# Retention and two Strassen MLPs: unit pairs read and combined a stage sooner, words loaded as staging frees, attention in halves

## The chip, the core and the metric

One core of a Trainium2 chip. TensorE multiplies, VectorE and ScalarE move and convert, GpSimd (POOL) and SyncE (SP) issue DMAs, each in its own order. The metric is the device time of one execution, in microseconds (us): lower is better.

## What is computed

The input of 4 batches, 8 heads, 768 positions and a head size of 64 goes through a retention (a linear attention with a decay per head), then two MLPs over 3072 tokens of width 512 with a hidden width of 2048, all in fp32:

```python
for t in range(S):
    state = gamma * state + einsum('bhd,bhe->bhde', k[:, :, t], v[:, :, t])
    y[:, :, t] = scale * einsum('bhd,bhde->bhe', q[:, :, t], state)
x = y.transpose(0, 2, 1, 3).reshape(B * S, H * D)
h = x @ w_in1;  x = np.maximum(0.01 * h, h) @ w_out1
h = np.maximum(x @ w_in2, 0.0);  return (h * h) @ w_out2
```

The weights come as 64-bit words (the doubles that numpy holds) and are turned into fp32 on the chip.

## The kernel before, in words

**Numbers.** Every fp32 operand is held as a high and a low part, and every product takes three matmuls (high by high, low by high, high by low): `product` (line 692) is 6 matmuls, for two tiles of depth. Tokens go in three blocks of 1024, each in two halves of 512.

**Phase one: retention, first block.** The launch runs 8 attention units. Then `begin_loop` (1141) and `plain_period(q)` (1189, q from 2 to 7) work through the 8 pairs of hidden blocks of the first layer. A period runs `emit_plain` (739, the products into the hidden layer, evacuated at line 720) and `put_out` (1120, which is 12 matmuls of `emit_out`, 768). Beside that it converts the words of the weights: `load_w` (316) loads 1 MB of them (w_in: two tiles tagged `sg`; w_out: two tiles in `xh2`, `xl2` or `xh7`, `xl7`), `scale_words` (367) makes two ScalarE passes, `shift`, `sign` and `add` (372 to 384) three VectorE passes, and `add` is the last to read the words. `combine` (444) forms the seven units of a pair (4 in tile wa: units 1, 5, 6, 3; 3 in tile wb: 7, 2, 4), and they are kept in HBM as `wid`. Each period from q = 3 also holds one attention unit (`group`, 1134).

`attend` (204) does the scores of one unit and the output of the unit before it: 16 pairs of small score matmuls mixed with the first half of `y`, then the increments mixed with the second half of `y`. `y` has one bank in PSUM after the launch; line 276 (VectorE) empties it and line 256 takes the scores. `group` then loads q, k and v (tiles `r`) for later units.

**The late loop** (1413) runs the 16 `emit_out` of the second token half, with a `group()` behind i = 0, 2, 5 and 8, `split_late(i + 2)` (splitting hidden tiles into `gh`, `gl` or `gg`) ahead, and words of w2, in 512 KB pieces (tiles `st`, `load_piece` 334): pieces 0 to 2 are loaded ahead of the loop, the rest by `next_piece` (1125), which also converts one piece.

**Phase two: Strassen.** Block 1 runs `strassen_period`. Blocks (0, 2), (1, 0), (1, 1) and (1, 2) (layer, block) run `both_block` (922). For each pair n it runs `first_half` (859: products 1, 5, 6, 3, with the banks `pa` and `pd` copied out by ScalarE at lines 865, 868, 871 and by VectorE at 874) and, between them, `second_half` of the pair before (878: products 7, 2, 4). The order on TensorE is 1, 7, 5, 2, 6, 4, 3, where 7, 2 and 4 belong to the pair before. Product 6 adds to the bank of product 1, and product 3 to that of product 5. `first_half` needs wa alone, `second_half` wb alone. `read_units` (808) loads both for pair n + 1 at the end of pair n; each has two buffers.

Then come seven stages of 48 matmuls (`STAGES`, order 1, 5, 6, 3, 7, 2, 4; n is the stage's number from 0, e its entry from 0 to 15), while VectorE and ScalarE prepare the next stage (`prepare`), and `read_stage` loads the weights of the stage after. Block (0, 2) also combines pairs 0 and 1 of the second layer there: `units_here` (811) loads the fp32 weights through POOL's queue (`store`), combines them in two steps and stores the units; pair 0 begins at (n, e) = (1, 1), pair 1 at (2, 13), both in the tile `xh4`. `operands` (664) prepares the seven operands of the next block in steps at the entries of the table `at`; its last read of `xs` frees that tile, into which block (1, 0) then loads (`made`, line 929, through SP).

**What sets the order.** TensorE's order is the order written (`mm` chains every matmul behind the last one). With `strict` on, so is that of VectorE and ScalarE (`seq`); the late loop and `both_block` are not strict, and there a list scheduler of the framework places the instructions, but within `aside()` (111) an instruction stays behind the last marked one. `load` issues on SP, `store` on POOL; both queues work in order, and an issue that waits for a tile holds up those behind it. A tile's next load waits until its last reader is done.

Of the kernel before, what the change touches and what calls it, by code (L numbers as in the profile page):

```python
# [17 lines left out]
P = 128  # L18
# [39 lines left out]
def retention_then_two_mlps(  # L58
# [74 lines left out]
    def mm(**kw):  # L133
        pin(nc.tensor.matmul(**kw))  # L134

    def load(**io):
        pin(nc.sync.dma_start(**io))  # L137

    def store(**io):
        pin(nc.gpsimd.dma_start(**io))  # L140
# [60 lines left out]
            return state[:, j + 1 - (c > 0)]  # L201
        return sts[n][:, k - 1]

    def attend(score=True, behind_mask=None):

        n = n_score[0] if score else NA
        m = n_done[0] if n_done[0] < n_score[0] else -1
# [36 lines left out]
        for one, two in (runs[0:2], runs[2:4]):  # L244
            for i in range(0, len(sets), 2):
                for kw in one[i:i + 2] + two[i:i + 2]:
                    mm(**kw)
        if n < NA:
            if c == 0:
                both = x_p.tile([P, 2, T], F32, tag=("xh7", "xl7", "xh2", "xl2")[n % 4], name="pm")  # L250
                pms[n] = both[:, 0]
                sts[n] = both[:, 1].rearrange("p (k b e) -> p k b e", k=4, b=2)
            else:
                pms[n] = a_p.tile([P, T], F32, tag="pm", name="pm", bufs=1)
                sts[n] = a_p.tile([P, 3, 2, D], F32, tag="st", name="st", bufs=1)
            seq(nc.vector.tensor_tensor(  # L256
                out=blocks(pms[n]), in0=blocks(sc), in1=mk[p].unsqueeze(1).to_broadcast([P, T // CH, CH]), op=ALU.mult,
            ))
            if c == 0:
                seq(nc.scalar.copy(memory(n, 1), inc[:, 0]))  # L260
# [55 lines left out]
    def load_w(q, half):  # L316
        if q >= NQ:
            return
        if half and q:
            t = [x_p.tile([P, 512], U64, tag=f"x{l}{2 if q % 2 else 7}", name="sg") for l in "hl"]  # L320
            for n in range(2):
                load(out=t[n], in_=w1[q, 1][:, 512 * n:512 * n + 512])
        else:
            t = w_p.tile([P, 1024], U64, tag="sg", name="sg", bufs=2)
            load(out=t, in_=w1[q, half])
        stage[q, half] = t
# [78 lines left out]
    def parts(t, k, n):  # L405
        return t.rearrange("p (k l n c) -> p k l n c", k=k, l=2, n=n)

    def put_in(lay, q, a, c):

        k = lay + 1  # L410
        a, c = parts(a, k, 4), parts(c, k, 3)
        win[lay, q] = {
            i: [
                [t[:, kt % k, l, m, kt // k * P:kt // k * P + P] for l in range(2)]
                for kt in range(2) for t, m in ((a, n - 3) if n >= 3 else (c, n),)
            ]
            for i, n in UNIT.items()
        }

    def open_in(q):  # L420

# [386 lines left out]
    def read_units(lay, q):  # L808
        read_wid(lay, q, *unit_tiles())

    def units_here(q, f, x=None):
        store(out=f, in_=wflt[q, 0])
        yield
        a, c = unit_tiles()
        put_in(1, q, a, c)
        steps = combine(f, a, c, 2, x)
        for _ in range(2 if x is None else 1):
            next(steps)
        if x is not None:
            put_wid(1, q, a, None)  # L820
        yield
        for _ in steps:
            pass
        put_wid(1, q, a if x is None else None, c)
# [97 lines left out]
    def both_block(lay, b, here):  # L922
# [4 lines left out]
        if here_too:  # L927
            v = quarters() + scratch("ss", "ss", "wb", "wf")
            made = make_units(5, *v[:5], put=load, apart=True)
            next(made)  # L930
        for n in range(NQ + 1):
            f = first_half(lay, b, n) if n < NQ else iter(())
            r = second_half(lay, b, n - 1, pa) if n else iter(())
            if here_too and 3 <= n <= 6:
                with aside():
                    next(here[n // 5], None)
            if here_too and n == NQ - 1:
                with aside():
                    next(made, None)
            for k in range(4):  # L940
                pa = next(f, None)
                if n == NQ - 1 and k < 2:
                    read_stage(lay, 0, (2 * k, 2 * k + 1))
                if lay == 0 and n and (k == 1 or k == 3 and n in (1, 2, 4, 5)):
                    with aside():
                        next(here, None)
                if k < 3:
                    next(r, None)
                if here_too and (n, k) in ((2, 0), (4, 0), (4, 2), (6, 0)):
                    with aside():  # L950
                        next(made, None)
            if n == NQ - 1:
                read_stage(lay, 1, range(4))
            if n and n + 1 < NQ and (not here_too or n not in (3, 5)):
                read_units(lay, n + 1)
            if here_too:
                if n in (1, 2, 4, 6):
                    with aside():
                        next(made, None)
                if n == 0:  # L960
                    here = [units_here(4, v[5], v[7]), units_here(6, v[6], v[5])]
                    for m in here:
                        next(m)
                elif n in (2, 4):
                    made = make_units(5 + n // 2, *v[:5], apart=True)
                    next(made)
        A = [ps["acc"].tile([P, T], F32, tag=f"acc{m}", name="acc") for m in range(2)]
        s = {}
        steps = None if nl is None else operands(nl, nb)
        at = {4: (7, 13), 5: (5, 11), 6: (1, 5, 9)} if lay else {4: (13,), 5: (5, 11), 6: (1, 4, 8, 12)}  # L970
        for n, i in enumerate(STAGES):
            if i in (5, 2):
                Dd = [ps["acc"].tile([P, T], F32, tag=f"acc{2 + m}", name="acc") for m in range(2)]
# [5 lines left out]
            for e, (q, m) in enumerate(order):  # L979
                r = rot[i, q]  # L980
                for k, (l, h) in enumerate(((0, 0), (1, 0), (0, 1))):
                    mm(
                        out=bank[m], lhsT=units[i, q // 2][:, q % 2, l, m * P:(m + 1) * P], rhs=r[:, h],
                        start=i in (1, 5, 2) and q == 0 and k == 0, stop=q == NQ - 1 and k == 2, skip_group_check=True,
                    )
                if e % 2 and n + 1 < len(STAGES):
                    prepare(STAGES[n + 1], q)
                if e == 1:
                    if 1 <= n <= 5:
                        read_stage(lay, n + 1, range(4))  # L990
                    if n == (1 if lay else 3) and nl is not None:
                        read_x(nb)
                    if n in (3, 5) and lay and nl is not None:
                        read_units(1, (n - 3) // 2)
                if lay == 0:
                    if (n, e) in ((0, 1), (0, 9), (0, 15)):
                        with aside():
                            next(here, None)
                    if (n, e) in ((1, 1), (2, 13)):
                        made = units_here(n - 1, x_p.tile([P, 1024], F32, tag="xh4", name="of"))  # L1000
                        next(made)
                    if n in (2, 4) and e in (3, 9):
                        with aside():
                            next(made, None)
                if steps and e in at.get(n, ()):
                    with aside():
                        next(steps, None)
# [123 lines left out]
            cast_piece(n)  # L1131
        n_piece[0] += 1

    def group():

        attend(n_score[0] < NA)
        n = n_score[0]
        value_loads_to(n + 1)
        loads_to(n + 2)

    def begin_loop(out):
# [14 lines left out]
        add(w, f)  # L1156
        store(out=wraw[2], in_=f)
        load_w(3, 0)
        o = hold_out(0)
        high_out(0, o)  # L1160
        low_out(0, o)
# [27 lines left out]
    def plain_period(q):  # L1189

        last = q == NQ - 1

        load_w(q + 2, 0)
        split_high(2 * q - 2)
        if not last:
            w, f = open_in(q + 1)
# [14 lines left out]
        if not last:  # L1211
            add(w, f)
            store(out=wraw[q + 1], in_=f)
        else:
            made = make_in(1, 0)
            next(made)
# [12 lines left out]
        for s, r in out:  # L1229
            add(s, r)  # L1230
        load_w(q + 2, 1)

        put_out(0, 2 * q - 2)
        if not last:
# [148 lines left out]
    for b in range(NB - 1):  # L1383
# [14 lines left out]
        if b == 0:  # L1398
            for _ in made:
                pass  # L1400
            sum_up(stage["of", NQ - 1])
            sums_high(NQ - 1)
            sums_low(NQ - 1)
            for n in range(3):
                load_piece(n)
        put_out(b, NJ - 2)
        put_out(b, NJ - 1)
        strict[0] = False
# [4 lines left out]
        for i in range(NJ):  # L1413
            if i + 2 < NJ:
                split_late(i + 2)
            emit_out(0, b, 1, 2 * LATE[i // 2] + i % 2, (0, 12), i == 0, i == NJ - 1)
            k = i // 2 + 3
            if i % 2 and k < NQ:
                read_out(LATE[k], spare if k % 3 == 2 else None)
            if b == 0 and i in (0, 2, 5, 8):  # L1420
                group()
                with aside():
                    prep_to(n_score[0] + 1)
            if b == 0 and i == 11:
# [98 lines left out]
```

## Time and profile before

| | us |
|---|---|
| median of 3 runs | 1061.63 (1057.16 to 1063.43) |
| profiled execution | 1057.65 |
| its span, first to last instruction | 1055.6 |

The profile is of that one execution. Times in its views are us from the span's start. PE is TensorE, DVE VectorE, ACT ScalarE; "L134" is line 134, where every matmul is recorded, so matmuls are told apart by their tiles. A wait names what ended it. The granted clock (PEclk) is a share of 2.4 GHz; over a stretch it is a mean of its two levels, 1.2 and 2.4.

### The profile page before, as it was taken

The page shows a single profiled execution, that of the slowest core. Times are in us where ns is not written, and L with a number is a line of the kernel's source. Part 1 is how long each engine was busy: PE and PEld are TensorE (multiplying, and loading weights), DVE is VectorE, ACT ScalarE, POOL GpSimd, SP SyncE. Part 2 cuts the span into 40 slices and gives each one's busy share as a digit, 9 for nine tenths or more (in the row PEclk, how much of TensorE's full clock was granted, in tenths as well). Part 3 has the DMA queues.
Part 4 walks back from the last instruction along what each step waited for, and adds up shares of the span by engine and source line. Part 5 has one row for each costly group of instructions (what it writes and reads, how often), then busy time and mean ns, then how long its engine had stood idle before and what let it go on. Part 6 is the DMA issues. An engine that isn't in the chain of part 4 may idle for free.

```text
span 1055.6 us, 18359 instructions
## 1 busy us (share of the span) xinstructions
PE 1026.1 (97%) x7133; PEld 842.1 (80%) x7133; DVE 764.4 (72%) x1273; ACT 586.0 (56%) x999; POOL 89.9 (9%) x155
## 2 busy tenths in 40 slices
PE   6899999899999999999999899999999999999998
PEld 5787888687877888887788688888888888888886
DVE  5796988777888759487888678868455958456953
ACT  4575664455566556476566466655455555455542
POOL 0010111101000000122011121001000001000000
PEclk8999999899999999999999999999999999999999
DMA  9688976998999878799896588975356784357461
GB/s 341 210 306 334 362 245 208 411 345 302 398 407 361 334 259 329 278 357 369 322 332 254 213 316 305 391 265 230 121 186 242 272 286 183 128 201 276 163 239 60
DMA packets 74277, 294.01 MB, mean 279 GB/s; under 512 B 8400, under 2 KB 8656, under 8 KB 63952
## 3 DMA queue, kind: packets, MB, share of 16 engines
q1 hardware_dynamic: 55536, 213.08, 55.6%
q0 software_dynamic: 18512, 79.70, 19.3%
q8 instruction: 56, 0.92, 0.3%
q14 instruction: 29, 0.24, 0.1%
q10 hardware_dynamic: 144, 0.07, 0.0%
HBM read 206.84 MB, written 85.98 MB: 277 GB/s over the span
## 4 chain that ended last, share of the span: by engine, by line
PE 84%; DMA 10%; DVE 3%; ACT 1%; SPq 1%; issue 1%; ACTq 0%; DVEq 0%
PE acc L134 43%; PE pa L134 25%; PE pd L134 9%; PE pb L134 5%; DMA wa<-wid 2%; DMA wf<-wraw 2%; DMA r<-first 2%; DMA st<-w 2%; DMA sg<-w 1%; PE y L134 1%; PE sc L134 1%; SPq L137 1%; DMA wo<-wpl 1%; PE inc L134 1%; DVE wa L396 0%
## 5 line engine op out<-in xcount | busy, mean ns | idle before, releaser
L134 PE MATMUL acc<-rot,wu 128*128 128x512 f32 x1344 | 308.3, 391 | 0.0
L134 PEld LDWEIGHTS acc<-rot,wu 128*128 128x128 f32 x1344 | 252.4, 188 | 55.3
L134 PE MATMUL pa<-xh,wa 128*128 128x512 f32 x576 | 180.1, 394 | 9.2 <-DMA wa<-wid 4.9
L847 DVE TENSOR_TENSOR rot<-gu,rot 128x512 fp32r<-128x512 f32 x160 | 109.3, 688 | 47.5 <-ACT rot L846 47.1
L846 ACT CAST rot<-gu 128x512 fp32r<-128x512 f32 x160 | 99.4, 621 | 77.0 <-PE acc L134 53.6
L134 PEld LDWEIGHTS pa<-xh,wa 128*128 128x128 f32 x576 | 107.8, 189 | 34.4 <-DMA wa<-wid 6.1
L134 PE MATMUL pa<-xl,wa 128*128 128x512 f32 x288 | 112.7, 391 | 0.0
L134 PE MATMUL acc<-gh,wo 128*128 128x512 f32 x400 | 104.8, 394 | 0.1
L134 PE MATMUL pa<-xh,wb 128*128 128x512 f32 x320 | 99.8, 393 | 0.5 <-DVE gt L881 0.5
L134 PE MATMUL pd<-xh,wa 128*128 128x512 f32 x320 | 98.5, 389 | 0.0
L134 PEld LDWEIGHTS acc<-gh,wo 128*128 128x128 f32 x400 | 74.5, 188 | 17.1 <-ACT gh L731 0.5
L134 PEld LDWEIGHTS pa<-xh,wb 128*128 128x128 f32 x320 | 59.5, 189 | 13.6 <-DVE gt L881 1.1
L134 PEld LDWEIGHTS pd<-xh,wa 128*128 128x128 f32 x320 | 60.1, 188 | 12.5
L847 DVE TENSOR_TENSOR rot<-gt,rot 128x512 fp32r<-128x512 f32 x64 | 44.1, 691 | 29.4 <-ACT rot L846 29.0
L134 PEld LDWEIGHTS pa<-xl,wa 128*128 128x128 f32 x288 | 54.3, 189 | 11.5
L134 PE MATMUL pa<-xl,wb 128*128 128x512 f32 x160 | 62.3, 389 | 0.0
L134 PE MATMUL pd<-xl,wa 128*128 128x512 f32 x160 | 62.2, 389 | 0.0
L846 ACT CAST rot<-gt 128x512 fp32r<-128x512 f32 x64 | 39.8, 622 | 38.7 <-DVE rot L847 27.1
L134 PE MATMUL acc<-gl,wo 128*128 128x512 f32 x200 | 56.8, 391 | 0.0
L711 ACT ACTIVATE gt<-gt 128x512 f32<-128x512 f32 x48 | 30.3, 632 | 45.3 <-DVE gt L874 32.5
L886 DVE TENSOR_TENSOR gu<-gu,pb 128x512 f32<-128x512 f32 x32 | 22.0, 687 | 41.3 <-PE pb L134 41.2
L134 PE MATMUL pb<-xh,wb 128*128 128x512 f32 x160 | 49.5, 391 | 0.8 <-DVE pm L256 0.8
(133 smaller groups left out, 1676.1 us busy)
## 6 DMA issues: line engine op xcount, KB each, us to landing
wu<-wou SPq DMA_DIRECT2D x100, 512.0 KB, 5.7
wa<-wid SPq DMA_DIRECT2D x28, 1024.0 KB, 7.3
wou<-of POOLq DMA_DIRECT2D x48, 512.0 KB, 6.7
wb<-wid SPq DMA_DIRECT2D x28, 768.0 KB, 5.9
wo<-wpl SPq DMA_DIRECT2D x20, 1024.0 KB, 7.9
r<-first SPq DMA_DIRECT2D x64, 256.0 KB, 8.0
st<-w SPq DMA_DIRECT2D x24, 512.0 KB, 9.0
wid<-wa POOLq DMA_DIRECT2D x12, 1024.0 KB, 8.9
```

The costliest lines, as they stand in the source:

```text
L134: pin(nc.tensor.matmul(**kw))
L137: pin(nc.sync.dma_start(**io))
L711: nc.scalar.activation(out=g, in_=g, func=AF.Relu)
L846: mark[0] = nc.scalar.copy(r[:, 0], s).ins
L847: mark[1] = nc.vector.tensor_tensor(out=r[:, 1], in0=s, in1=r[:, 0].bitcast(F32), op=ALU.subtract).ins
L886: nc.vector.tensor_tensor(out=u[:, 0], in0=u[:, 0], in1=pb, op=ALU.add)
```

## The change

1. `load_w(q, 0)` for the words of w_in: `load_w(4, 0)` goes right behind `load_w(3, 0)`, and a period's load of pair q + 2 at its start becomes a load of pair q + 3 behind its `add`.
2. Pieces 0 to 2 of the words of w2 are loaded in the last period, behind its last `add`, and no longer ahead of the last two `put_out`.
3. In the late loop `group` stands around `emit_out(i)`: scores and the first half of y, then the 12 matmuls, then increments and the rest of y, then the loads.
4. In `both_block` the order becomes 1, 5, 7, 6, 3, 2, 4. wa of pair n + 2 is read behind product 3 of pair n, wb of pair n + 1 at the end of pair n.
5. In block (0, 2) pair 1 of the second layer begins at (1, 3) in a tile of its own (`xh5`), both pairs are loaded through SP, and their steps are at stages 2 and 3 instead of 2 and 4. The steps of `operands` for the first layer move in `at`.
6. In block (1, 0) the first step of `made` goes from the start of the block to the end of pair 0.

```diff
-    def attend(score=True, behind_mask=None):
+    def attend(score=True, behind_mask=None, between=None):
...
             for i in range(0, len(sets), 2):
                 for kw in one[i:i + 2] + two[i:i + 2]:
                     mm(**kw)
+            if between and one is runs[0]:
+                between()
...
+    def read_part(lay, q, second):
+        if q < NQ:
+            n, tag = (3, "wb") if second else (4, "wa")
+            t = late["p"].tile([P, 512 * n], F32R, tag=tag, name=tag, bufs=2)
+            o = 2048 if second else 0
+            load(out=t.bitcast(F32), in_=wid[lay, q][:, o:o + 512 * n])
+            put_part(lay, q, t, second)
-    def units_here(q, f, x=None):
-        store(out=f, in_=wflt[q, 0])
+    def units_here(q, f, x=None, put=store):
+        put(out=f, in_=wflt[q, 0])
...
             made = make_units(5, *v[:5], put=load, apart=True)
-            next(made)
...
-                if k < 3:
+                if k == 1:
+                    next(r, None)
+                if k == 3:
+                    if not here_too or n not in (2, 4):
+                        read_part(lay, n + 2, 0)
+                    next(r, None)
                     next(r, None)
...
-            if n and n + 1 < NQ and (not here_too or n not in (3, 5)):
-                read_units(lay, n + 1)
+            if n and (not here_too or n not in (3, 5)):
+                read_part(lay, n + 1, 1)
...
                 if n == 0:
+                    next(made)
                     here = [units_here(4, v[5], v[7]), units_here(6, v[6], v[5])]
...
-        at = {4: (7, 13), 5: (5, 11), 6: (1, 5, 9)} if lay else {4: (13,), 5: (5, 11), 6: (1, 4, 8, 12)}
+        made = []
+        at = {4: (7, 13), 5: (5, 11), 6: (1, 5, 9)} if lay else {4: (5, 13), 5: (3, 8, 13), 6: (3, 9)}
...
-                    if (n, e) in ((1, 1), (2, 13)):
-                        made = units_here(n - 1, x_p.tile([P, 1024], F32, tag="xh4", name="of"))
-                        next(made)
-                    if n in (2, 4) and e in (3, 9):
+                    if (n, e) in ((1, 1), (1, 3)):
+                        f = x_p.tile([P, 1024], F32, tag="xh4" if e == 1 else "xh5", name="of")
+                        made.append(units_here(e // 2, f, put=load))
+                        next(made[-1])
+                    if n in (2, 3) and e in (3, 9):
                         with aside():
-                            next(made, None)
+                            next(made[n - 2], None)
...
         load_w(3, 0)
+        load_w(4, 0)
...
-        load_w(q + 2, 0)
         split_high(2 * q - 2)
...
             add(w, f)
             store(out=wraw[q + 1], in_=f)
+            load_w(q + 3, 0)
...
         load_w(q + 2, 1)
+        if last:
+            for n in range(3):
+                load_piece(n)
...
             sums_low(NQ - 1)
-            for n in range(3):
-                load_piece(n)
...
-            emit_out(0, b, 1, 2 * LATE[i // 2] + i % 2, (0, 12), i == 0, i == NJ - 1)
+            def out_here():
+                emit_out(0, b, 1, 2 * LATE[i // 2] + i % 2, (0, 12), i == 0, i == NJ - 1)
+            attends = b == 0 and i in (0, 2, 5, 8)
+            if attends:
+                group(out_here)
+            else:
+                out_here()
             k = i // 2 + 3
             if i % 2 and k < NQ:
                 read_out(LATE[k], spare if k % 3 == 2 else None)
-            if b == 0 and i in (0, 2, 5, 8):
-                group()
+            if attends:
                 with aside():
                     prep_to(n_score[0] + 1)
```

`put_in` is split into `put_part`, called once for wa and once for wb; it only names parts of tiles and issues nothing. `group` hands `between` to `attend`.

## Rows read from the trace of the kernel before

**Rows 1.** The page: busy us, share of the span and instructions of each engine.

```profile
PE 1026.1 (97%) x7133; PEld 842.1 (80%) x7133; DVE 764.4 (72%) x1273; ACT 586.0 (56%) x999; POOL 89.9 (9%) x155
```

**Rows 2.** Waits of TensorE: who waited, for whom, total us, times, longest us.

```profile
PE sc L134 <- issue: 6.2, 3, 2.9
PE pa L134 <- DMA wa<-wid: 4.9, 2, 3.8
PE y L134 <- DVE xs L276: 3.7, 1, 3.7
PE pa L134 <- ACT g L720: 2.6, 1, 2.6
```

**Rows 3.** ScalarE in order of time: start, us, engine, line [idle before <-releaser].

```profile
92.47 1.12 ACT L369 ACTIVATE wf<-sg 128x1024 f32<-128x1024 f32 x1 [9.66 <-DMA sg<-w]
```

**Rows 4.** Chain that ended last, 60 to 125: start us, us, what.

```profile
77.12 15.24 DMA sg<-w
...
95.14 3.01 PE pa L134 x12
```

**Rows 5.** VectorE in order of time near 60: the add of pair 2.

```profile
58.87 1.23 DVE L384 CUSTOM_DVE_ANT_0 wf<-sg,wf 128x2048 uint16<-128x2048 uint16 x1
```

**Rows 6.** TensorE in order of time, 196 to 201.

```profile
196.62 0.33 PE L134 MATMUL sc<-r 64*64 64x64 f32 x4
200.66 0.37 PE L134 MATMUL y<-pm,r 64*64 64x64 f32 x2 [3.71 <-DVE xs L276]
```

**Rows 7.** VectorE in order of time, 188 to 201 (nine instructions left out before the last).

```profile
188.77 0.69 DVE L736 TENSOR_TENSOR gg<-g,gg 128x512 fp32r<-128x512 f32 x1
193.11 0.43 DVE L374 TENSOR_SCALAR sf<-sf 128x512 uint32<-128x512 uint32 x1 [3.64 <-ACT sf L369]
...
199.93 0.68 DVE L276 TENSOR_TENSOR xs<-y,tabs 128x512 f32<-128x512 f32 x1
```

**Rows 8.** Chain that ended last, 176 to 232.

```profile
179.97 15.97 DMA st<-w
...
204.34 9.34 PE acc L134 x36
...
213.69 0.20 PE sc L134 x2
...
215.71 8.48 PE acc L134 x36
```

**Rows 9.** Stretches: length, busy us (instructions) by engine, PEclk, DMA share, GB/s.

```profile
165.00:180.00 15.00, 15.00 (x186) 12.39 (x185) 11.09 (x22) 10.54 (x19) 1.45 (x2) 1.00 0.43 156
195.00:210.00 15.00, 11.29 (x157) 9.39 (x156) 13.76 (x25) 6.43 (x11) 0.00 (x0) 0.77 1.03 412
240.00:255.00 15.00, 14.91 (x176) 11.89 (x174) 9.31 (x16) 7.47 (x13) 3.22 (x6) 1.00 0.75 245
255.00:285.00 30.00, 29.26 (x238) 24.12 (x239) 24.77 (x53) 19.85 (x39) 1.06 (x2) 1.00 1.02 386
```

**Rows 10.** Chain that ended last, the two waits for unit tiles.

```profile
465.54 10.80 DMA wa<-wid
476.38 3.06 PE pa L134 x12
...
593.61 12.18 DMA wa<-wid
605.83 4.40 PE pa L134 x12
...
612.95 2.72 PE pa L134 x12
```

**Rows 11.** POOL's queue in order of time, 586 to 600.

```profile
591.10 0.54 POOL L140 DMA_DIRECT2D wid<-wa  x1 [31.91 <-DVE wa L396]
...
592.16 3.22 POOL L140 DMA_DIRECT2D ydr<-ss  x6
```

**Rows 12.** ScalarE in order of time: the copy behind a product 1.

```profile
593.95 0.59 ACT L865 COPY gu<-pa 128x512 f32<-128x512 f32 x1 [1.58 <-PE pa L134]
```

More of the change, by code (lines that the diff above doesn't have):

```diff
@@ L408, in put_in, with put_part @@
     def put_in(lay, q, a, c):
+        put_part(lay, q, a, 0)
+        put_part(lay, q, c, 1)
+    def put_part(lay, q, t, second):
         k = lay + 1
[L411 to L418, printed above, removed]
+        t = parts(t, k, 4 - second)
+        if not second:
+            win[lay, q] = {}
+        for i, n in UNIT.items():
+            if (n < 3) == bool(second):
+                m = n if second else n - 3
+                win[lay, q][i] = [
+                    [t[:, kt % k, l, m, kt // k * P:kt // k * P + P] for l in range(2)] for kt in range(2)
+                ]
     def open_in(q):
@@ L1132, in next_piece, with group @@
         n_piece[0] += 1
-    def group():
-        attend(n_score[0] < NA)
+    def group(between=None):
+        attend(n_score[0] < NA, between=between)
         n = n_score[0]
```

## The prediction, made before the change was run

> **What bounds the kernel now.** I read the page first: TensorE is busy 1026.1 us, 97% of the span, VectorE 72% and ScalarE 56% [rows 1]. So TensorE's work sets the time, and a change that takes no matmul away can win at most the 29.5 us in which TensorE is idle, and what a lowered clock costs beside them. The view of waits then says which idle time can go. The largest group, 6.2 us ahead of the scores with no engine as its releaser, belongs to the launch, which the diff does not touch; 4.9 us wait for unit tiles from HBM, 3.7 for one VectorE instruction, 2.6 for one ScalarE instruction [rows 2]. Those three are 11.2 us in four places, and the change has a part for each. The chain of waits and the lists of single engines say what stood behind each place.
>
> **Place one, 92 us.** TensorE waits 2.6 us for the evacuation L720. ScalarE works in order, and ahead of that evacuation it stood 9.66 us at a conversion of w_in words [rows 3], whose load was issued at 77.12 and landed 15.24 us later [rows 4]. That is `load_w(4, 0)`, at the head of period 2. The change puts it right behind `load_w(3, 0)`. Its staging tile is free once the add of pair 2 has ended, at 60.1 [rows 5]; on SP's queue it passes only `load_w(3, 1)`, which waits for a later add anyway, and the loads of q, k and v. Even a landing of 15.24 us then ends at 75.4, 17 us before the conversion began: **2.6 us go**. Later words move forward by half a period; each waits on SP for the add of its own period, and behind it stand only loads that wait for work after that add. The loads that are passed land up to one 1 MB transfer later; their first user on TensorE is the attention in the next period, so I cost that at nothing.
>
> **Place two, 196 to 214 us.** The second attention of the late loop starts at 196.62; its y matmuls wait until 200.66 for L276, which empties the single y bank [rows 6]. VectorE had stood idle 3.64 us for words of w2 and then ran ten instructions, from 193.11 up to L276 at 199.93 [rows 7]; the words took 15.97 us to land [rows 8], with the DMA engines full (1.03) [rows 9]. Behind the wait the granted clock falls: 0.77 is the mean from 195 to 210 [rows 9], a spell at the lower of its two levels (1.2 GHz, against 2.4 before the wait). Attention and 36 output matmuls take 7.72 + 9.34 us here, and 2.02 + 8.48 at the next one [rows 6, 8]: the place costs 5.7 + 0.9 = **6.6 us**.
>
> Two parts bear on it. First, the loads of pieces 0 to 2 move from behind the loop of periods into the last period, ahead of the loads of its attention. Piece 0 needs xh7, free since period 6, and goes out nearly a period sooner; pieces 1 and 2 need xh2 and xl2, which the add of period 7 frees, a few us sooner, and SP stands there with only that attention's loads behind it, which wait for TensorE anyway. The DMA engines are 43% busy from 165 to 180 [rows 9], so all three should be in by 183, and VectorE's 3.64 us go. What passes behind them (four r loads, one `wo`) is late by up to 1 MB; each has its user more than 5 us off.
>
> Second, attention in halves: scores and the first part of y now stand ahead of `emit_out(i)`, increments and the rest of y behind it. TensorE's sum is the same. But y is wanted 12 matmuls, 2.8 us (8.48 over 36, times 12), sooner, and is complete no sooner: old, two `emit_out` passed between the attention at i = 0 and the next one; new, one. If VectorE keeps its list, the ten instructions start at 189.5, behind the one at 188.77 [rows 7], and reach L276 6.8 us later, at 196.3, while y is wanted at 193.8 (2.8 before 196.62): a wait of 2.5 us, with `emit_out(2)` queued behind it. If the list is drawn up anew with L276 further forward, the wait is nil. Between 0 and 2.5, plus at worst 2.9 for the clock (6.6 less 3.7), I take 2.0, nearer to the list that the rows show, and no clock: the 2.6 us wait at 92 had its twelve matmuls done in 3.01 us [rows 4], while the 3.8 us wait at 606 had them in 4.40 [rows 10]. **Gain 4.6**, bounds 1.2 and 6.6.
>
> **Place three, 476 us.** In `both_block` the tile wa of the next pair is asked for when product 3 of the pair before the running one is done. Asked for at 465.54, it landed 10.80 us later, TensorE had waited 1.1 us, and the twelve matmuls behind took 3.06 instead of 2.72 [rows 2, 10]: **1.4 us**. New: wa is read alone, ahead of wb, behind product 3, and the order 1, 5, 7, 6, 3, 2, 4 puts two products of 1.36 us behind product 3. The lead grows from 9.5 to 12.2 us, over the 10.8: the 1.4 us go. wb, behind it on SP, waits for product 4 anyway, and keeps nine products between its release and its use.
>
> **Place four, 594 to 610 us.** Block (1, 0) waits 3.8 us for wa of pair 2 and then runs twelve matmuls in 4.40 instead of 2.72 us [rows 2, 10]: **5.4 us**. The tile was asked for at 593.61, behind another load on SP that waited for the operands; beside its 12.18 us two unit stores (1.75 MB) and six output stores were in flight, all released together from 591.10 because POOL's queue had stood 31.91 us behind the combining of pair 1 [rows 11]. New: pair 1 is loaded from SP into a tile of its own and combined in stage 3, after pair 0 in stage 2, so those stores leave long before; and the other load goes behind wa. wa can be asked for at 592.6, when product 3 of pair 0 is done, and is wanted at 602.1. At 10.80 us it would be 1.3 us late, at 12.18 2.7 us; with those stores gone I take no wait: gain 5.4, lower bound 2.7.
>
> The Trainium skill ("DMA: Bandwidth & Descriptors", Anatomy of one DMA) gives 2.0 us plus the bytes at 436 GB/s, an estimate of 4.4 us for 1 MB. By that neither the old load nor the new would be late and place four would cost nothing today; the trace disagrees, with 10.80 and 12.18 us [rows 10], and the sum goes by the rows.
>
> **What is added.** Both combinings (some 4 us of VectorE each) and the operand steps come sooner, into stages where VectorE is fuller, and the first step comes closer to the load of xs; every prepared tile has a stage of 11 us ahead of its use, which covers it; without that cover, up to 4 us. In the new order products 1 and 5 have two products (2.72 us) instead of three before their bank is added to again; the copy between takes 0.59 us, and ScalarE stood idle 1.58 us waiting for the product [rows 12]: covered. `put_part`, the tile xh5 and two loads moved from POOL to SP cost TensorE nothing.
>
> **Sum.** 2.6 + 4.6 + 1.4 + 5.4 = 14.0. From 255 to 285 the DMA engines are full (1.02), and TensorE will come 7 us sooner; 240 to 255 has 3.75 us of slack (0.75) [rows 9] and the early pieces take 3.7 us of transfers out, so I let only 1 us be given back: 13.0. The profiled execution took 1057.65 us, so 1044.6. The median of the three runs is 4.0 higher, 1061.63; I keep some two thirds of that offset, since part of it will be late landings at the same places: **1047 us**.
>
> **Rivals.**
> *The DMA engines are the bound from 180 to 345.* For: shares above 1.0 and landings of 10 to 16 us. Against: TensorE waits little there. Then the 7.2 us of places one and two come back as late words: 1054. The Trainium skill ("DMA: Bandwidth & Descriptors", Issuing engines are not separate DMA queues) says that issuing from another engine saves only sequencer time; by that rule this rival holds. Chance 0.17.
> *The y bank takes the place of the words.* The wait is 2.5 us or more and the clock falls again: only 1.2 of the 4.6 is won, 1050. Chance 0.13.
> *The loads do not come sooner* (pieces held by their tiles, wa by product 3): 3.4 us of place two and 2.7 of place four are not won and 5 instead of 1 are given back: 10.1 on the forecast, 1057. Chance 0.08.
> *Slower: the copies behind products 1 and 5.* ScalarE's order puts waits for VectorE ahead of them, and 1.36 us of room is gone in each of 32 pairs (four blocks of eight). It decides from 0.44 us a pair (14.0 over 32); at 0.6 us a pair, 19 us on the forecast, 1066. Against: [rows 12]. Chance 0.07.
>
> **Numbers.** The forecast has 0.55. Less than 0.5%, 5.3 us, cannot be told from no change here. Faster: forecast, y bank and most of the first rival, 0.80; same: the rest of it and the third, 0.13; slower: 0.07. Low end: all four places in full (16.0) off 1057.65 is 1041.6, and 2.6 for the other places; the high end takes in the third rival with 2 us to spare: 1039 to 1059.
>
> **What would show it.** Right: no wait for L720 near 90; pieces landed before 183; a wait at L276 of 0 to 2.5 us with the clock kept; no wait for wa; POOL's stores of pair 1 before 580. Wrong: a spell of half clock between 180 and 210, new waits from 250 to 345, or waits of `pa` or `pd` for the copies L865 and L868 in the blocks.

## The result, and the profile after

The changed kernel takes 1048.3 us (median of 6 runs, 1046.33 to 1049.93) against 1061.95 (6 runs): a ratio of 0.9874, 95% interval 0.9852 to 0.9896. Its profiled execution took 1046.89 us with a span of 1045.1, on the fast side of its runs; the one before took 1057.65. Lines have moved: L720 is L728 now, L276 is L278, L369 is L371, L731 is L739, L704 is L712, and the copies L865 and L868 are L882 and L885.

The page of the changed kernel, busy time of each engine:

```profile
PE 1025.5 (98%) x7133; PEld 840.7 (80%) x7133; DVE 765.4 (73%) x1273; ACT 587.8 (56%) x999; POOL 88.5 (8%) x153
```

TensorE's work is the same as in [rows 1]; what has shrunk is its idle time, from 29.5 us to 19.6. Its waits, changed kernel:

```profile
PE acc L134 <- DMA wu<-wpl: 1.9, 1, 1.9
...
PE acc L134 <- ACT rot L863: 0.8, 1, 0.8
...
PE y L134 <- DVE xs L278: 0.4, 1, 0.4
```

Of the groups of [rows 2] the waits for wa and for the evacuation are gone, and the one for the y bank is 0.4 us instead of 3.7. The first two lines here are new.

TensorE runs the same matmuls. Where their order was changed, it is back in step at the ends of the stretches below, so the start of the matmul with the same number in TensorE's list can be compared (starts are the first column of the timeline). Stretches in us:

| stretch, by its starts before / after | before | after | saved |
|---|---|---|---|
| launch, to 41.12 / 41.70 | 39.66 | 40.24 | -0.58 |
| place one, to 95.14 / 92.95 | 54.02 | 51.25 | 2.77 |
| other plain periods, to 179.99 / 177.67 | 84.85 | 84.72 | 0.13 |
| place two, to 225.36 / 218.38 | 45.37 | 40.71 | 4.66 |
| Strassen periods, to 349.46 / 341.99 | 124.10 | 123.61 | 0.49 |
| twelve output matmuls at 342, to 352.67 / 345.21 | 3.21 | 3.22 | -0.01 |
| to 459.68 / 452.27 | 107.01 | 107.06 | -0.05 |
| place three, to 506.70 / 497.83 | 47.02 | 45.56 | 1.46 |
| stages 0 to 4 of block (0, 2), to 564.70 / 555.47 | 58.00 | 57.64 | 0.36 |
| start of stage 5, to 570.42 / 564.40 | 5.72 | 8.93 | -3.21 |
| to 601.23 / 595.26 | 30.81 | 30.86 | -0.05 |
| place four, to 620.27 / 608.86 | 19.04 | 13.60 | 5.44 |
| the rest, to 1051.54 / 1040.66 | 431.27 | 431.80 | -0.53 |

The four places bring 14.33 us, and 3.21 of them are lost again at one spot that the prediction did not name. The chain of waits shows it (start, us, what):

```profile
541.31 19.10 DMA wu<-wpl
560.41 0.14 issue
560.55 3.05 PE acc L134 x12
563.59 0.02 issue
563.62 0.02 ACTq L863
563.63 0.04 issue
563.67 0.63 ACT rot L863
564.30 0.10 issue
564.40 5.75 PE acc L134 x24
```

The second weight tile of stage 5 took 19.10 us to land. Beside it POOL's queue (changed kernel, in order of time) let two unit pairs go:

```profile
541.23 0.55 POOL L140 DMA_DIRECT2D wid<-wa  x1 [5.12 <-DVE wa L398]
541.77 0.55 POOL L140 DMA_DIRECT2D wid<-wb  x1
548.98 0.53 POOL L140 DMA_DIRECT2D wid<-wa  x1 [6.66 <-DVE wa L398]
549.50 0.53 POOL L140 DMA_DIRECT2D wid<-wb  x1
```

In [rows 11] pair 1's stores left at 591.10, ahead of block (1, 0). Now they leave at 548.98, while the 2 MB of xs (issued at 540.42) and six weight tiles of 512 KB are in flight. The Trainium skill ("DMA: Bandwidth & Descriptors", Issuing engines are not separate DMA queues) has it that DMAs run on the same 16 DMA engines and interleave, whichever engine started them; the trace agrees, with POOL's stores beside SP's 19.10 us.

Place two in the changed kernel, VectorE in order of time:

```profile
191.54 0.69 DVE L278 TENSOR_TENSOR xs<-y,tabs 128x512 f32<-128x512 f32 x1
```

TensorE in order of time:

```profile
192.28 0.27 PE L134 MATMUL y<-pm,r 64*64 64x64 f32 x2 [0.44 <-DVE xs L278]
```

The stretch there (columns as in [rows 9]), with the granted clock at 1.00 (2.4 GHz), where it had been 0.77:

```profile
195.00:210.00 15.00, 15.00 (x243) 11.90 (x242) 10.76 (x21) 7.33 (x12) 0.00 (x0) 1.00 1.03 413
```

### The profile page after: what moved, and what is told of

Same layout as the page of the kernel before. It is cut to its first block, busy times and chain, and to the rows that moved or that the text cites. A ratio compares the mean times of both kernels' runs of the same rounds, so it can differ in the third digit from the quotient of the medians.

```text
span 1045.1 us, 18366 instructions
## 1 busy us (share of the span) xinstructions
PE 1025.5 (98%) x7133; PEld 840.7 (80%) x7133; DVE 765.4 (73%) x1273; ACT 587.8 (56%) x999; POOL 88.5 (8%) x153
## 4 chain that ended last, share of the span: by engine, by line
PE 90%; DMA 5%; DVE 3%; ACT 1%; issue 1%; SPq 0%; DVEq 0%; ACTq 0%
PE acc L134 42%; PE pa L134 29%; PE pd L134 10%; PE pb L134 5%; DMA wu<-wpl 2%; DMA r<-first 2%; PE y L134 1%; PE sc L134 1%; DMA wf<-wraw 1%; PE inc L134 1%; DMA wu<-wou 0%; DVE wa L398 0%; DVE gl L744 0%; DVE wf L380 0%; DVE wf L386 0%
## 5 line engine op out<-in xcount | busy, mean ns | idle before, releaser
L891 DVE TENSOR_TENSOR gt<-gt,pd 128x512 f32<-128x512 f32 x32 | 22.0, 686 | 56.7 <-PE pd L134 48.1
L744 DVE TENSOR_TENSOR gl<-g,gh 128x512 fp32r<-128x512 f32 x50 | 34.2, 687 | 23.4 <-ACT gh L739 20.8
```

Of the source, the lines that this page charges most:

```text
L744: mark[1] = seq(nc.vector.tensor_tensor(out=gl, in0=g, in1=gh.bitcast(F32), op=ALU.subtract)).ins
L891: nc.vector.tensor_tensor(out=t[:, 0], in0=t[:, 0], in1=pd, op=ALU.add)
```

## Experiments

Each kernel is the changed one with one edit, unless said otherwise. The columns are the stretches of the table above in the profiled execution of each; the medians come from 4 to 12 runs.

| kernel | median | one | two | at 342 | three | stage 5 | four |
|---|---|---|---|---|---|---|---|
| before | 1061.95 | 54.02 | 45.37 | 3.21 | 47.02 | 5.72 | 19.04 |
| changed | 1048.3 | 51.25 | 40.71 | 3.22 | 45.56 | 8.93 | 13.60 |
| c1_again (the changed kernel) | 1049.2 | 51.29 | 40.72 | 7.97 | 45.55 | 10.55 | 13.60 |
| v11_words_behind (the same) | 1049.4 | 51.28 | 40.72 | 3.53 | 45.79 | 9.88 | 13.60 |
| u1_whole_attention | 1047.9 | 51.28 | 39.41 | 4.33 | 46.18 | 8.70 | 13.60 |
| u2_pieces_late | 1054.1 | 51.22 | 44.62 | 4.26 | 45.84 | 8.34 | 13.60 |
| u3_pair1_late | 1045.0 | 51.26 | 40.76 | 3.22 | 45.68 | 5.73 | 14.31 |
| v10_late_pair_words_behind (as u3) | 1046.4 | 51.27 | 40.76 | 3.22 | 46.72 | 5.72 | 14.50 |
| u4_stage5_first | 1045.7 | 51.29 | 40.71 | 4.40 | 46.52 | 5.73 | 13.60 |
| u5_old_order | 1050.4 | 51.26 | 40.76 | 4.57 | 47.72 | 8.71 | 13.60 |
| u6_words_late | 1054.7 | 52.90 | 40.87 | 5.43 | 47.03 | 9.48 | 13.60 |
| u7_made_first (u3 and one edit) | 1048.4 | 51.27 | 40.72 | 8.16 | 46.82 | 5.73 | 15.97 |
| u9_steps_stage4 | 1046.8 | 51.30 | 40.71 | 7.18 | 46.43 | 5.72 | 13.60 |
| w1_late_pair_words_behind (u3 and one edit) | 1045.7 | 51.27 | 40.72 | 4.10 | 45.39 | 5.72 | 14.31 |

Read down a column: "one", "two" and "four" hold to 0.2 us and move only where an edit touches them. "At 342" and, less, "three" change from execution to execution; so does "stage 5", from 8.3 to 10.6, as long as its tile is late.

### The late loop: halves and pieces

```diff
-            if attends:
-                group(out_here)
-            else:
-                out_here()
+            out_here()
...
             if attends:
+                group()
```

> The changed kernel with the attention of the late loop whole again, behind emit_out; all other parts stay. Theory (the early pieces win place two, the halves only ask for y 2.8 us sooner): no wait at the y bank from 185 to 215, attention and output matmuls at full clock, time equal to the changed kernel's 1048.3 us or up to 1 us less. Rival (the halves win part of place two, since the list of VectorE was drawn up anew around them): a wait of 1 us or more at the y bank again, 1050 to 1053 us.

Measured: 1047.9 us, ratio 0.9886 (0.9849 to 0.9924): not told apart from the changed kernel by its time. The stretch of place two is 1.3 us shorter without the halves. TensorE waits for the y bank nowhere from 185 to 215. The halves do not win the place; they cost a little there.

```diff
-        if last:
-            for n in range(3):
-                load_piece(n)
...
             sums_low(NQ - 1)
+            for n in range(3):
+                load_piece(n)
```

> The changed kernel with the words of pieces 0 to 2 loaded behind the loop of periods, as before; halves stay. Theory (the late words are what fills place two): pieces land between 187 and 197, VectorE stands idle 2 to 4 us for them, TensorE waits 3 us or more for the emptying of the y bank and the clock falls behind it: 4 to 7 us above the changed kernel, 1052 to 1055 us. Rival (the halves and the new list carry it): TensorE's wait at the y bank stays under 1 us, within 1 us of 1048.3.

Measured: 1054.1 us, ratio 0.9941 (0.9916 to 0.9967). VectorE of this kernel in order of time:

```profile
189.71 0.43 DVE L376 TENSOR_SCALAR sf<-sf 128x512 uint32<-128x512 uint32 x1 [2.47 <-ACT sf L371]
```

Its TensorE in order of time:

```profile
194.66 0.37 PE L134 MATMUL y<-pm,r 64*64 64x64 f32 x2 [2.99 <-DVE xs L278]
...
196.56 2.62 PE L134 MATMUL acc<-gh,wo 128*128 128x512 f32 x8
```

VectorE stands for the words again, the y bank is emptied late, and eight output matmuls behind the wait take 2.62 us (2.11 in the changed kernel). Of place two's 4.66 us, 3.91 go back. The early pieces carry the place. The median rose by 5.8, more than this stretch; the rest was not traced to a place.

### The words of w_in

```diff
-        load_w(4, 0)
...
+        load_w(q + 2, 0)
         split_high(2 * q - 2)
...
-            load_w(q + 3, 0)
```

> The changed kernel with the words of w_in loaded at the head of a period for pair q + 2 again, and load_w(4, 0) not ahead of the loop. Theory: TensorE waits 2 to 3 us for the evacuation at line 712 near 92 us again, since ScalarE stands behind the conversion of words that land 15 us after their issue; nothing else moves: 2.6 us above 1048.3, 1050.5 to 1051.5 us. Rival (the later loads of the loop matter too, or what is won at 92 is given back by 345): the difference at 345 us from the start is under 1 us, or over 4.

Measured: 1054.7 us, ratio 0.9956 (0.9935 to 0.9977). ScalarE of this kernel in order of time:

```profile
93.35 1.13 ACT L371 ACTIVATE wf<-sg 128x1024 f32<-128x1024 f32 x1 [8.52 <-DMA sg<-w]
```

Its TensorE in order of time:

```profile
96.04 0.74 PE L134 MATMUL pa<-xh,wa 128*128 128x512 f32 x2 [1.47 <-ACT g L728]
```

The mechanism of place one is back, with 1.65 us of its 2.77 in this execution. The median lies 6.4 above the changed kernel's, well over the 2.6 expected. In the trace there are 2.2 more at 342, 1.5 in place three, 0.6 at stage 5 and 1.4 in the launch. At the matmul that starts at 345.21 in the changed kernel it is 6.0 us behind, over the 4 that the rival named. But executions of one program differ there too: the changed kernel and c1_again by 4.75 at 342, 1.6 at stage 5 and 1.3 in the launch, u3 and v10 by 1.0 in place three. Whether the late words cause the rest stays open.

### Stage 5 and block (1, 0)

```diff
-                    if (n, e) in ((1, 1), (1, 3)):
...
+                    if (n, e) in ((1, 1), (2, 13)):
+                        made = units_here(n - 1, x_p.tile([P, 1024], F32, tag="xh4", name="of"))
+                        next(made)
+                    if n in (2, 4) and e in (3, 9):
...
```

> The changed kernel with both pairs of the second layer loaded and combined in block (0, 2) at the old places (pair 1 from stage 2, entry 13, steps in stage 4, through POOL's queue, tile xh4); product order and reads by parts stay. Theory (the stores of pair 1, 33 us sooner against TensorE, crowd the unit weights of stage 5, and cost the 3 us lost from 553 to 566): no wait for those weights near 560, so 3 us come back, but in block (1, 0) the first wa tile is late again by 1 to 3 us, with or without a lowered clock behind it: 1047 to 1051 us. Rival A (xs and eight weight loads going out at once crowd themselves): the wait near 560 stays at 1.5 us or more. Rival B (the reading of wa behind product 3 alone settled place four): no wait for wa, 1045 to 1046 us.

Measured: 1045.0 us, ratio 0.9864 (0.9828 to 0.9900). POOL's queue of this kernel in order of time:

```profile
550.32 0.55 POOL L140 DMA_DIRECT2D wid<-wa  x1 [16.06 <-DVE wa L398]
...
579.24 0.54 POOL L140 DMA_DIRECT2D wid<-wa  x1 [26.07 <-DVE wa L398]
```

Its chain of waits at the first wa that block (1, 0) asks for, that of pair 2:

```profile
582.84 9.85 DMA wa<-wid
592.70 0.04 issue
592.74 1.66 PE pa L134 x6
```

Stage 5 is back at 5.73 us, and place four loses only 0.7. So what u3 takes back had cost 3.2 us there and returned 0.7 here. It takes back both pairs (pair 0's stores leave at 550.32 instead of 541.23); u9 below moves the combining of pair 1 alone. Rival B came closest.

```diff
-                    if 1 <= n <= 5:
+                    if 1 <= n <= 5 and (lay or n != 4):
                         read_stage(lay, n + 1, range(4))
+                    if n == 3 and not lay:
+                        read_stage(lay, 5, range(4))
```

> The changed kernel with the four unit weight loads of stage 5 of block (0, 2) issued ahead of the 2 MB load of xs instead of behind it; nothing else. Theory (the order in which DMAs go out decides who is late): the second of them lands before 555 instead of at 560.4, no wait near 560 and none of the 0.8 us behind it, 3 us less: 1045 to 1046 us. Rival (the engines are full and the lateness only moves): xs lands 3 us or more later, the rotations behind its first conversion are late, a wait for ScalarE of 1 to 3 us from 555 to 570: 1047 to 1049 us.

Measured: 1045.7 us, ratio 0.9858 (0.9827 to 0.9889), stage 5 at 5.73. The second tile was issued at 539.90 and landed at 544.90; xs landed at 559.59 instead of 550.04, 9.5 us later, and TensorE waited for nothing from 540 to 580. The order of issue decided who was late, and xs could afford it.

```diff
-                    if n in (2, 3) and e in (3, 9):
+                    if n in (2, 4) and e in (3, 9):
                         with aside():
-                            next(made[n - 2], None)
+                            next(made[n // 2 - 1], None)
```

> The changed kernel, pair 1 loaded early through SP into its own tile as in the change, but combined in stage 4 as before the change instead of in stage 3. Theory (what costs 3 us near 560 are the 1.75 MB of pair 1's stores beside xs and the weights of stage 5): those stores go out after 556, the weights of stage 5 land in time, no wait near 560; the stores are in by 580, so no wait for wa either: 1044.5 to 1045.5 us. Rival (the stores then crowd the weights of stage 6): a wait of 1 us or more between 564 and 578, 1046 to 1048 us.

Measured: 1046.8 us, ratio 0.9895 (0.9859 to 0.9931), from 1043.5 to 1052.8; stage 5 at 5.72, place four at 13.60. Both places come out as expected; the 7.18 us at 342 in this execution lie ahead of the edit. Three different ways of keeping pair 1's stores, or xs, away from the weights of stage 5 give the same 3.2 us back.

```diff
             made = make_units(5, *v[:5], put=load, apart=True)
+            next(made)
...
-                    next(made)
```

> The kernel of u3_pair1_late (1045.0 us, old places of the two pairs) with the load of pair 5 in block (1, 0) issued ahead of the first wa again, as before the change. Theory (place four was won by the order of two loads on SP, not by stores that leave sooner): the 0.5 MB load ahead, held for the operands, makes wa land 1 to 2.5 us later than 592.7, a wait of 1.4 to 3 us, with a lowered clock from some 2.6 us on: 1046.5 to 1049.5 us. Rival (the lead is enough by itself): wait under 0.8 us, 1045 to 1045.5 us.

Measured, on the base of u3: 1048.4 us, ratio 0.9900 (0.9874 to 0.9927). The chain of waits of this kernel:

```profile
588.98 0.02 issue
589.00 11.51 DMA wa<-wid
600.51 0.04 issue
600.55 1.65 PE pa L134 x6
```

The landing takes 11.51 us instead of 9.85 and TensorE waits 2.07; place four takes 1.66 us more than in u3. Counted from the start of the stretch "four", wa was asked for at the same point in both kernels, so that much is due to the order of two loads on SP. Where the rest of the median's 3.4 comes from was not measured; the stretch at 342 took 8.16 in this execution.

```diff
-                if k == 1:
-                    next(r, None)
-                if k == 3:
-                    if not here_too or n not in (2, 4):
-                        read_part(lay, n + 2, 0)
-                    next(r, None)
+                if k < 3:
                     next(r, None)
...
-            if n and (not here_too or n not in (3, 5)):
-                read_part(lay, n + 1, 1)
+            if n and n + 1 < NQ and (not here_too or n not in (3, 5)):
+                read_units(lay, n + 1)
```

> The changed kernel with the old order of products (1, 7, 5, 2, 6, 4, 3) and wa and wb of a pair read together at the end of the pair before; all else stays. Theory (the order wins the lead of wa and nothing else): in block (0, 2) a wait for wa of about 1 us near 470 is back with up to 0.4 us of slower matmuls behind it; in block (1, 0) the lead of the first tile is 9.5 us in either order and its landing 6 us, so no wait there; 1.4 us above the changed kernel's 1048.3, 1049 to 1050.5 us. Rival (the closer products 1 and 6, 5 and 3 cost time on the copies in every pair): 1045 us or less.

Measured: 1050.4 us, ratio 0.9922 (0.9892 to 0.9953). The chain of waits of this kernel in block (0, 2):

```profile
459.13 11.55 DMA wa<-wid
470.68 0.04 issue
470.73 3.01 PE pa L134 x12
```

Place three is back (47.72), with the wait of 1.6 us and slower matmuls behind it. Place four stays at 13.60: with pair 1's stores gone, the old order is enough there. The 0.36 us of stages 0 to 4 go back as well (58.00). Behind place four the closer products cost nothing that shows, for the rest of the run is no shorter in the old order (432.19 against 431.80); in place three they do cost something at times, as the part on the rivals shows.

### The stretch at 342

> The changed kernel itself once more, on the chip of the next two. Theory (the transfers from 255 to 345 are so dense that the w2 words for the conversion near 340 land at a different time in each execution; the profiled one was a good draw): another wait for the split at line 739 near 342, between 0 and 5 us with what it slows, and single times that spread over 4 us or more around 1048. Rival (the waits of 1 to 3 us seen there in the experiments come from their edits): no wait there, spread under 3 us.

Measured: 1049.2 us, ratio 0.9888 (0.9854 to 0.9922), single times from 1046.2 to 1054.9. The chain of its profiled execution, which was the slowest of its runs:

```profile
330.94 13.52 DMA st<-w
...
344.55 0.66 ACT xs L371
345.21 0.57 ACT st L372
345.78 0.52 ACT g L728
...
346.32 0.63 ACT gh L739
346.95 0.04 issue
347.00 4.61 PE acc L134 x12
```

w2 words were issued at 330.94 and landed 13.52 us later. ScalarE works in order: behind their conversion stand the activation and the split for twelve output matmuls. TensorE waited 2.9 us, and then ran them in 4.61 at a mean clock of 0.63 (length, busy us by engine, clock, DMA share, GB/s):

```profile
347.00:351.60 4.60, 4.60 (x13) 3.65 (x14) 3.62 (x9) 3.35 (x8) 0.00 (x0) 0.63 0.72 258
```

The same program in its first profile had the load issued at 328.45 and landed at 339.24, and waited nothing. So 0 to 5 us there are a matter of the execution. The issue itself is late as well: in no trace here are more than 8 of SP's DMAs in flight, and in both executions the words went out just behind the landing of the DMA eight before them (at 328.43 and at 330.93), so one late landing delays a later issue.

```diff
-        begin(n + 1)
+        if q < NQ - 2:
+            begin(n + 1)
...
         split_rest(j0)
+        if q >= NQ - 2:
+            begin(n + 1)
+            finish(n + 1)
```

> The changed kernel; in the last but one period of block 1 the conversion of the second piece of w2 words goes behind the split of that period's hidden tile, on ScalarE and VectorE, instead of ahead of it. Theory (ScalarE's order puts the split, and with it 12 output matmuls, behind a load that is late): no wait for line 739 near 342, whenever the words land; the output matmuls take the same 3.2 us in every execution, 1 to 2 us below the unedited kernel of this call, 1046 to 1047.5 us, with the slow single times gone. Rival (the words only hold up something else of the next period, such as the copies of products at line 712): no difference beyond 0.5 us.

> Both remedies on the changed kernel: the pairs of block (0, 2) at their old places (u3_pair1_late) and the conversion behind the split (v11_words_behind). Theory (the two are 200 us apart and add): no wait at 342, none at 560, a wait of 0.4 us for the first wa in block (1, 0): 3 us below v11_words_behind, 1043 to 1044.5 us. Rival (what is won at 342 is given back at the next late transfer before 560): within 1 us of 1045.0, the time of u3_pair1_late.

The edit missed: periods 6 and 7 have no piece to convert, the conversion in question is that of period 5, and every engine's list came out as without the edit. Measured: 1049.4 (0.9889, 0.9855 to 0.9923) and 1046.4 (0.9856, 0.9828 to 0.9885), to be read as second measurements of the changed kernel and of u3. With them the changed kernel has 18 runs with a median of 1048.8, and u3 has 12 with a median of 1046.0.

```diff
-        begin(n + 1)
+        if q != 5:
+            begin(n + 1)
...
         split_rest(j0)
+        if q == 5:
+            begin(n + 1)
+            finish(n + 1)
```

> The kernel of u3_pair1_late with the conversion that stands at 340 us (period 5 of block 1, the only period near there that has one) behind the split at line 739. The edit of v11 and v10 sat one period later, where there is no piece to convert, so those two were the unedited kernels again. Theory (ScalarE's order puts the split behind a late load): no wait for line 739 near 342, the twelve output matmuls there take 3.2 us whenever the words land, the slow single times go: median 1044 to 1045.5 us against 1045.0 and 1046.4 of the same kernel without the edit, no run above 1047. Rival (the late words then hold up the copies at line 712 or the unit conversion at line 395 of the next period): a wait of 1 us or more for one of these from 345 to 360, no gain.

Measured: 1045.7 us, ratio 0.9859 (0.9828 to 0.9890), one run at 1050.1. Inconclusive: the words landed early enough in the profiled execution (at 341.08) that the edit had nothing to save. The stretch at 342 took 4.10 all the same, with a wait of 0.60 for the copy at line 712, the rival's line, at 347.15. And a wait of the kind that the edit was to take away stood a period earlier:

```profile
308.62 2.11 PE L134 MATMUL acc<-gh,wo 128*128 128x512 f32 x8 [1.47 <-ACT gh L739]
```

The late words strike in whichever period they land late; moving one conversion does not take the spread away.

## Why the prediction was right, and where it was not

**Place one.** 2.6 us were forecast, 2.77 measured. The waiting conversion was the cause: put back, its wait for words and TensorE's wait for L728 are there again.

**Place two.** 4.6 forecast, 4.66 measured, from two errors that cancel. The pieces landed at 167.0, 177.1 and 180.2, ahead of the 183 of the text. The wait that was to remain, 2.0 us, is 0.44: VectorE's list was drawn up anew and L278 begins at 191.54, not after ten instructions. The landing of 15.97 us in [rows 8], which ended at 195.94, is also not that of the words for which VectorE had stood idle until 193.11; those had landed at 192.39, after 12.95 us. Nothing in the sum hangs on it. But the step "TensorE's sum is the same" failed. A whole attention takes 2.02 us and the 36 output matmuls beside it 8.49. In halves they are 1.09 + 1.09 and 2.94 + 5.75, so 0.4 us more each time. With the attention whole (u1) the stretch saves 5.96. That the total agrees is luck.

**Place three.** 1.4 forecast, 1.46 measured, and the undone order brings the wait back. But this was one of the better executions: over the twelve traces with the new order the stretch takes 46.1 on average, 0.9 less than in the one trace before. The rivals below say why.

**Place four.** 5.4 forecast, 5.44 measured, but the reason given was only one of several. "With those stores gone I take no wait" holds with the old order too (u5); there the load that was to go behind wa was out at 582.45, wa itself at 589.85, and it held nothing up. With the stores left at their old place (u3) the rest of the change already brings 4.7. Of this, 1.7 is the order of the two loads (u7). The new order of products has no visible part: counted back from the start of the stretch "four", wa was asked for 7.62 us ahead in the kernel before and 8.65 us ahead in every other kernel, u5 among them. The remaining 3.1, of u7 against the kernel before, was not divided further: in u7 wa goes out 1.0 us sooner against TensorE and pair 1's stores 2.1 us sooner, the wait is 2.07 us instead of 3.8, and the clock stays. The 4.4 us that the prediction works out from the Trainium skill ("DMA: Bandwidth & Descriptors", Anatomy of one DMA) come from a fit for DMAs that GpSimd issues, while wa is loaded through SP, beside full DMA engines (share 1.00 from 465 to 477 and from 593 to 606), so the 10.80 and 12.18 us do not test that fit.

**The step that failed** stands under "What is added": "Both combinings ... come sooner", costed on VectorE alone, with "those stores leave long before" set down as a gain. The 1.75 MB that pair 1 stores were moved out of one crowded stretch into another, and nothing was said of what was in flight there. They cost 3.2 us at stage 5: u9, which moves only the combining of pair 1 and its stores, brings them back, as u3 and u4 do in other ways.

**What is given back.** 1 us was put at 255 to 285. That stretch gave back nothing in the profiled execution. The first rival (late words from 180 to 345) is true in part, further on: the wait at 342 takes 0 to 5 us of an execution. On the scale of the profiled execution the forecast was 1044.6 and the time 1046.89: 2.2 of the 2.3 us between them are stage 5 (3.2, where 1.0 was allowed, and for another place); the other differences of the table, of 0.6 us at most each, nearly cancel. The offset to the median, taken as 2.4, is 1.4.

**The other rivals.** The y bank did not take over and the loads did come sooner. The slower case, copies late behind products 1 and 5 in every pair, is refuted by u5's remainder. But "covered", read from a copy in block (1, 0) [rows 12], does not hold everywhere in block (0, 2), where ScalarE has conversions to do as well. In eight of the twelve traces with the new order TensorE waits once in place three, 0.2 to 1.1 us, for a copy L882 or L885; in the two with the old order it does not there. In u4 (0.9 us) the copy stands behind a conversion that waits for words, in u6 behind two conversions of unit weights. ScalarE and TensorE of u6, each in order of time:

```profile
496.49 1.14 ACT L395 CAST of<-of 128x512 fp32r<-128x512 f32 x2
497.53 0.58 ACT L882 COPY gu<-pa 128x512 f32<-128x512 f32 x1
```

```profile
498.16 0.73 PE L134 MATMUL pa<-xh,wa 128*128 128x512 f32 x2 [1.13 <-ACT gu L882]
```

Each of these waits is shorter than the 1.36 us of room that the new order gave up. So the rival's mechanism is real, once in a run and not 32 times, and it goes with "three" from execution to execution: 45.4 to 45.7 without such a wait, 47.03 with the longest.

**A better version.** u3 (the unit pairs at their old places, all else as changed) and u4 (the weights of stage 5 ahead of xs) both lie some 3 us below the changed kernel by their medians (for u3, 1046.0 against 1048.8 with all runs of either program taken together); the trace shows where: the 3.2 us at stage 5.

## What to carry to other kernels

A store that is moved sooner must be costed where it lands: list the transfers in flight at its new time, and the first reader behind each. Where two parts of a change are meant for the same wait, undo them one at a time, since each may be enough and one may cost something elsewhere. When TensorE waits for less, the next late load decides, and its time varies from one execution to the next: compare the starts of the same matmuls over several profiles before a microsecond is put down to an edit.

## What was not expected of the hardware

The length of a single wait did not decide whether the clock fell. In u9, around a wait of 2.16 us that ended at 347.57, the granted clock came down from 1.00 (stretches; columns as above):

```profile
340.00:346.00 6.00, 5.41 (x24) 4.13 (x22) 3.32 (x11) 1.49 (x4) 0.00 (x0) 1.00 1.02 416
346.00:349.00 3.00, 1.43 (x3) 1.17 (x4) 2.83 (x6) 2.97 (x7) 0.00 (x0) 0.75 0.74 293
349.00:352.00 3.00, 3.00 (x11) 2.40 (x10) 2.06 (x5) 1.93 (x5) 0.00 (x0) 0.68 0.84 320
```

In u7, around a wait of 2.07 us that ended at 600.55, it stayed:

```profile
598.30:603.00 4.70, 2.63 (x12) 2.03 (x12) 4.13 (x8) 2.73 (x5) 0.00 (x0) 1.00 1.01 422
```

Before the change, the twelve matmuls behind the wait of 2.6 us at 92 had taken 3.01 us, near the 2.72 of an undisturbed twelve [rows 4, 10]. So the "lowered clock from some 2.6 us on" that u7 expected is not borne out. What the chip does at such waits was not settled here.
